# Retention and a mixture of experts: blocks of 768 slots with products of branched width, in place of blocks of 256

## The chip, the cores and the metric

The kernel runs on one core of a Trainium2 chip, in float32. The metric is the device time of one execution in microseconds (us). Each kernel ran in turn with the kernel before on the same chip. The experiments were made in three rounds, on chip 2, chip 3 and chip 2 again; across rounds, ratios and the block stages of the profiles compare better than times. A core's engines are named as in the profile: PE is the matrix engine (PEld its weight loads), DVE, ACT and POOL the vector, scalar and general engines, SP the engine that issues most transfers. PEq and the like are the profile's names for their sequencers.

## The reference

Retention over 8 sequences of 576 tokens (8 heads of 64) gives x with 512 features for each of 4608 tokens. A gate then picks one of 8 experts for each token, and the token goes through that expert's two matrices:

```python
for s in range(S):
    fresh_e = int(np.argmax(logits[b, s]))
    if s == 0 or local_gate[b, s] < 0.5:
        e = fresh_e
    else:
        e = prev_e if prev_e >= 0 else fresh_e
    prev_e = e
    ...                                        # p: softmax of the logits
    h = np.maximum(x[b, s] @ w1[e], 0.0)       # w1[e]: 512 x 1024
    out[b, s] = p[e] * (h @ w2[e])             # w2[e]: 1024 x 512
```

How many tokens an expert gets is known only when the kernel runs. With these inputs it is 652, 576, 581, 554, 591, 517, 606 and 531.

## The kernel before

Three stages follow each other: retention, which writes x to DRAM; routing, which gives each token a slot in a list that is sorted by expert; and the blocks, in which slots are gathered, go through their expert, and are scattered to their rows of the output. Each expert's tokens are padded to whole blocks of T = 256 slots. There are always as many blocks as any choice of experts can need, and nothing branches:

```python
T = 256
SUB = T // P                       # P = 128
NBLK = (NTOK - E) // T + E         # 25

for j in range(NBLK):
    e = nc.values_load(eid[0:1, j:j + 1], engines=[ET.SP], ...)
    w1s = weights.tile(...); w2s = weights.tile(...)      # two buffers each
    # cut: eight transfers of 512 KB, that expert's w1 and w2
    for u in range(SUB):
        # cut: gather 128 rows of x, transpose them on PE into PSUM (xgps)
        nc.vector.tensor_copy(xT[:, :, u * P:(u + 1) * P], xps)
    hT = mid.tile([P, FK, T], F32, name="hT")
    for m in range(0, FK, 2):                             # FK = 8
        hps = ps_h.tile([P, 2, T], F32, name="hps")
        for v in range(2):
            for c in range(DK):                           # DK = 4
                nc.tensor.matmul(hps[:, v, :], lhsT=w1s[:, m + v, c, :], rhs=xT[:, c, :], ...)
        nc.scalar.activation(hT[:, m:m + 2, :], hps, Act.Relu)
    for u in range(SUB):
        yps = ps_y.tile([P, D], F32, name="yps")
        for m in range(FK):
            nc.tensor.matmul(yps, lhsT=hT[:, m, u * P:(u + 1) * P], rhs=w2s[:, m, :], ...)
        nc.vector.tensor_scalar(y, yps, pslot[:, s:s + 1], None, Alu.mult)
        # cut: scatter y to its rows of out
```

Below, a "hidden product" is one into hps, an "output group" is the work on 128 slots into one yps tile, and a "seam" is the way from one block into the next.

Of the kernel before, what the change touches and what calls it, by code (L numbers as in the profile page):

```python
# [9 lines left out]
F32 = mybir.dt.float32  # L10
BF16 = mybir.dt.bfloat16
I32 = mybir.dt.int32
# [13 lines left out]
NTOK = B * S  # L26
NCH = NTOK // P  # chunks of 128 tokens
PER = 2 * S // P  # chunks in a pair of sequences
MID = PER // 2  # the chunk that ends one sequence and begins the next
HALF = S - P * MID  # L30
assert HALF == P // 2 and NTOK % (2 * S) == 0

T = 256  # tokens of one expert that go through its weights together
SUB = T // P
# Each expert's tokens are padded to whole blocks: what any choice of experts can need.
NBLK = (NTOK - E) // T + E
NSUB = NBLK * SUB
NOWHERE = 2 * NTOK  # the row of a slot without a token


@with_exitstack
def kernel(
# [23 lines left out]
    pslot = keep.tile([P, NSUB], F32, name="pslot")  # L66
    eid = keep.tile([1, NBLK], I32, name="eid")
    lt = keep.tile([P, NCH, E + 1], F32, name="lt")
    make_identity(nc, ident)

# [1 line left out]
    with ExitStack() as part:  # L72
# [12 lines left out]
        nc.scalar.dma_start(out=wg.rearrange("p k e -> p (k e)"), in_=wgl)  # L85
        # A key at partition p is seen from the queries at p and after.
        mask = once.tile([P, P], F32, name="mask")
# [44 lines left out]
        def outputs(i):  # L132
# [9 lines left out]
            if m > 0:  # L142
                # In the chunk of two sequences, only the first one's queries see what was before.
                n = HALF if m == MID else P
                for c in range(HP):
                    nc.tensor.matmul(  # L146
                        ops[0:n, 2 * c:2 * c + 2, :].rearrange("p h d -> p (h d)"),
                        lhsT=qT[:, c, 0:n], rhs=states[(i + 1) % 2][:, c, :],
                        start=False, stop=True, skip_group_check=True)
# [38 lines left out]

# [1 line left out]
    with ExitStack() as part:  # L190
# [12 lines left out]
        def for_all(t, n):  # L203
# [5 lines left out]
        one_of_sub = number("one_of_sub", [P, NSUB], [[1, NSUB]])  # L209
        one_of_blk = number("one_of_blk", [1, NBLK], [[1, NBLK]])  # L210
        token1 = number("token1", [P, NCH], [[P, NCH]], base=1, channel=1)
        place = number("place", [P, NCH], [[E * P, NCH]], base=1, channel=E)
# [10 lines left out]

        # The first of the greatest logits, and where the local gate asks for it.
        lg = lt[:, :, :E]
# [13 lines left out]
        nc.vector.memset(fr[HALF:HALF + 1, MID:NCH:PER], 1.0)  # L239
        # 8 * token + expert where it is asked for, -1 elsewhere: the last one that was is the  # L240
        # greatest until then.
        nc.vector.tensor_scalar(a, a, -1.0, float(E), Alu.mult, Alu.add)
# [29 lines left out]

        # Its share of the softmax.
        one = rt.tile([P, NCH, E], F32, name="one")
# [11 lines left out]

        # Tokens of each expert before each token: in its chunk, in the chunks before, and the
        # slots of the experts before.
        inside = ps_r.tile([P, NCH, E], F32, name="inside")
# [9 lines left out]
            cum.rearrange("p e c -> p (e c)"), going.rearrange("p e c -> p (e c)"),  # L299
            tot.rearrange("p e c -> p (e c)"), 0.0, Alu.mult, Alu.add)  # L300
        nb = rt.tile([P, E], F32, name="nb")
        nbi = rt.tile([P, E], I32, name="nbi")
        nc.vector.tensor_scalar(nb, cum[:, :, NCH - 1], float(T - 1), None, Alu.add)
        nc.vector.tensor_copy(nbi, nb)
        nc.vector.tensor_scalar(nbi, nbi, T.bit_length() - 1, None, Alu.arith_shift_right)
        nc.vector.tensor_copy(nb, nbi)
        last = rt.tile([P, E], F32, name="last")
        nc.vector.tensor_tensor_scan(last, nb, nb, 0.0, Alu.add, Alu.max)
        first = rt.tile([P, E], F32, name="first")
        nc.vector.tensor_tensor(first, last, nb, op=Alu.subtract)  # L310
        nc.vector.tensor_scalar(first, first, float(T), None, Alu.mult)
        nc.vector.tensor_tensor(cum, cum, tot, op=Alu.subtract)
        nc.vector.tensor_tensor(cum, cum, first.unsqueeze(2).to_broadcast([P, E, NCH]), op=Alu.add)
# [10 lines left out]

        # The expert of each block.
        past = rt.tile([1, NBLK, E], F32, name="past")
# [4 lines left out]
        nc.vector.tensor_scalar(eb, eb, float(E - 1), None, Alu.min)  # L331
        nc.vector.tensor_copy(eid, eb)

        # The token and the share of each slot: one product of the tokens' rows and columns.
        col = rt.tile([P, NCH, 2, NSUB], F32, name="col")
# [24 lines left out]

# [1 line left out]
    io = pool(ctx, "io", 4)  # L362
    mid = pool(ctx, "mid", 2)
    ps_x = pool(ctx, "ps_x", 2, PSUM)
    ps_h = pool(ctx, "ps_h", 3, PSUM)
    ps_y = pool(ctx, "ps_y", 3, PSUM)
    CUT = 4
    for j in range(NBLK):
        e = nc.values_load(eid[0:1, j:j + 1], engines=[ET.SP], min_val=0, max_val=E - 1,
                           skip_runtime_bounds_check_because="it is cut off there")  # L370
        w1s = weights.tile([P, FK, DK, P], F32, name="w1s")
        w2s = weights.tile([P, FK, D], F32, name="w2s")
        f = FK // CUT
        for t, src in ((w1s.rearrange("p m k f -> p (m k f)"), w1), (w2s.rearrange("p m d -> p (m d)"), w2)):
            for i in range(CUT):
                cols = slice(i * f * D, (i + 1) * f * D)
                nc.sync.dma_start(out=t[:, cols],
                                  in_=src[bass.ds(e, 1)].rearrange("o p x -> (o p) x")[:, cols])
        xT = mid.tile([P, DK, T], F32, name="xTs")
        for u in range(SUB):  # L380
            s = j * SUB + u
            xg = io.tile([P, D], F32, name="xg")
            nc.gpsimd.indirect_dma_start(  # L383
                out=xg, out_offset=None, in_=xd,
                in_offset=bass.IndirectOffsetOnAxis(ap=gidx[:, s:s + 1], axis=0))
            xps = ps_x.tile([P, DK, P], F32, name="xgps")
            for c in range(DK):
                nc.tensor.transpose(xps[:, c, :], xg[:, c * P:(c + 1) * P], ident)  # L388
            nc.vector.tensor_copy(xT[:, :, u * P:(u + 1) * P], xps)  # L389
        hT = mid.tile([P, FK, T], F32, name="hT")  # L390
        for m in range(0, FK, 2):
            hps = ps_h.tile([P, 2, T], F32, name="hps")
            for v in range(2):
                for c in range(DK):
                    nc.tensor.matmul(hps[:, v, :], lhsT=w1s[:, m + v, c, :], rhs=xT[:, c, :],  # L395
                                     start=(c == 0), stop=(c == DK - 1), skip_group_check=True)
            nc.scalar.activation(hT[:, m:m + 2, :], hps, Act.Relu)  # L397
        for u in range(SUB):
            s = j * SUB + u
            yps = ps_y.tile([P, D], F32, name="yps")  # L400
            for m in range(FK):
                nc.tensor.matmul(yps, lhsT=hT[:, m, u * P:(u + 1) * P], rhs=w2s[:, m, :],  # L402
                                 start=(m == 0), stop=(m == FK - 1))
            y = io.tile([P, D], F32, name="y")
            nc.vector.tensor_scalar(y, yps, pslot[:, s:s + 1], None, Alu.mult)  # L405
            nc.gpsimd.indirect_dma_start(  # L406
                out=out, out_offset=bass.IndirectOffsetOnAxis(ap=sidx[:, s:s + 1], axis=0),
                in_=y, in_offset=None, bounds_check=NTOK - 1, oob_is_err=False)


def _by_token(a, np):
    # (B, H, S, DH) -> (chunk, token, h d)
    return a.transpose(0, 2, 1, 3).reshape(NCH, P, D)


def _by_feature(a, np):
    # (B, H, S, DH) -> (chunk, d of two heads, pair token)
    x = a.transpose(0, 2, 1, 3).reshape(NCH, P, HP, P)
    return x.transpose(0, 3, 2, 1).reshape(NCH, P, D)


def _decay(np):
    """By each place in a pair of sequences and each head: what scales a query, and a key."""
    at = (np.arange(PER)[None, :] * P + np.arange(P)[:, None]) % S
    gamma = 1.0 - 2.0 ** (-5.0 - np.arange(H))
    power = gamma[None, None, :] ** at[:, :, None].astype(np.float64)
    both = np.stack([power / math.sqrt(DH), 1.0 / power], 1)
    return both.reshape(P, 2 * PER * H).astype(np.float32)
# [28 lines left out]
```

## Time and profile before

| | before |
|---|---|
| time, median of 3 runs | 1039.18 us (1037.77 to 1045.94) |
| PE busy, of a span of 1037.5 us | 974.9 us, 94% |
| first hidden product starts | 295.17 us |
| last output product ends | 1026.3 us |
| data moved | 166.03 MB |

The third and fourth rows frame the block stage: 731 us, which is 25 blocks of 29.25. Read the span first, then which engine is busy in each stretch. Here that is PE throughout the block stage, so a change there is worth the PE time it saves, less the PE idle time that it makes. The lines that carry this stand in the prediction.

### The profile page before, as it was taken

The page shows a single profiled execution, that of the slowest core. Times are in us where ns is not written, and L with a number is a line of the kernel's source. Part 1 is how long each engine was busy: PE and PEld are TensorE (multiplying, and loading weights), DVE is VectorE, ACT ScalarE, POOL GpSimd, SP SyncE. Part 2 cuts the span into 40 slices and gives each one's busy share as a digit, 9 for nine tenths or more (in the row PEclk, how much of TensorE's full clock was granted, in tenths as well). Part 3 has the DMA queues.
Part 4 walks back from the last instruction along what each step waited for, and adds up shares of the span by engine and source line. Part 5 has one row for each costly group of instructions (what it writes and reads, how often), then busy time and mean ns, then how long its engine had stood idle before and what let it go on. Part 6 is the DMA issues. An engine that isn't in the chain of part 4 may idle for free. (4 is left out here: it accounts for less than half of the span.)

```text
span 1037.5 us, 12062 instructions
## 1 busy us (share of the span) xinstructions
PE 974.9 (94%) x4918; PEld 719.0 (69%) x4918; DVE 166.8 (16%) x282; ACT 123.8 (12%) x238; POOL 140.7 (14%) x158
## 2 busy tenths in 40 slices
PE   7999999996479999999999999999999999999995
PEld 6999999995466666666666666666666666666662
DVE  2333332324711111010111111010111110010100
ACT  2222222221000000000000000000000000000000
POOL 2111111110021111011111110011111110110000
PEclk9999999998589999999999999999999999999998
DMA  5444444430735544555455544555455544555300
GB/s 201 154 158 157 151 163 162 163 133 32 273 122 203 201 156 148 185 197 177 153 179 187 193 156 153 181 193 188 138 187 203 164 158 160 195 183 167 127 2 0
DMA packets 47509, 166.03 MB, mean 160 GB/s; under 512 B 7006, under 2 KB 7134, under 8 KB 47456
## 3 DMA queue, kind: packets, MB, share of 16 engines
q1 hardware_dynamic: 39168, 142.62, 40.5%
q0 software_dynamic: 8000, 22.56, 6.3%
q8 instruction: 39, 0.64, 0.2%
q14 instruction: 14, 0.11, 0.0%
q10 hardware_dynamic: 288, 0.09, 0.0%
HBM read 146.37 MB, written 22.54 MB: 163 GB/s over the span
## 5 line engine op out<-in xcount | busy, mean ns | idle before, releaser
L395 PE MATMUL hps<-xTs,w1s 128*128 128x256 f32 x1600 | 353.2, 382 | 14.1 <-DVE xTs L389 14.1
L402 PE MATMUL yps<-w2s,hT 128*128 128x512 f32 x800 | 347.4, 592 | 0.0
L395 PEld LDWEIGHTS hps<-xTs,w1s 128*128 128x128 f32 x1600 | 303.0, 191 | 60.2 <-DVE xTs L389 19.8
L402 PEld LDWEIGHTS yps<-w2s,hT 128*128 128x128 f32 x800 | 152.0, 190 | 180.7 <-issue 179.4
L405 DVE TENSOR_SCALAR y<-yps,pslot 128x512 f32<-128x512 f32 x50 | 37.5, 751 | 665.4 <-PE yps L402 665.4
L397 ACT ACTIVATE hT<-hps 128x512 f32<-128x512 f32 x100 | 59.7, 597 | 700.2 <-PE hps L395 700.2
L406 POOL DMA_INDIRECT out_dram<-y,sidx x50 | 50.7, 1014 | 512.0 <-DVE y L405 505.3
L139 PE MATMUL ops<-vs,sT 128*128 128x64 f32 x576 | 82.3, 277 | 0.0
L139 PEld LDWEIGHTS ops<-vs,sT 128*128 128x128 f32 x576 | 72.4, 191 | 4.9 <-issue 0.6
L127 DVE TENSOR_TENSOR sT<-sps,mask 128x512 f32<-128x512 f32 x72 | 46.4, 686 | 159.9 <-PE sps L123 159.9
L383 POOL DMA_INDIRECT xg<-xd,gidx x50 | 48.7, 975 | 164.0 <-PE xgps L388 121.2
L116 POOL TENSOR_TENSOR vs<-ld,dec 128x512 f32<-128x512 f32 x36 | 37.5, 1042 | 190.0 <-PE kv L155 173.2
L123 PE MATMUL sps<-ld,kT 64*128 64x128 f32 x576 | 43.2, 288 | 0.2 <-DVE sT L127 0.2
L161 ACT COPY state<-kv 64x256 f32<-64x256 f32 x64 | 23.4, 366 | 160.2 <-PE kv L155 159.4
L176 PE MATMUL lps<-wg,xT 128*128 128x9 f32 x288 | 38.0, 259 | 1.5 <-ACT xT L174 1.1
L176 PEld LDWEIGHTS lps<-wg,xT 128*128 128x128 f32 x288 | 34.9, 191 | 5.2 <-ACT xT L174 4.7
L123 PEld LDWEIGHTS sps<-ld,kT 64*128 64x128 f32 x576 | 36.3, 190 | 2.9 <-DVE sT L127 0.4
L388 PEld LDWEIGHTS xgps<-ident,xg 128*128 128x128 f32 x200 | 24.2, 146 | 20.1 <-issue 19.5
L155 PE MATMUL kv<-vs,ld 128*128 128x128 f32 (+1 forms) x256 | 35.5, 281 | 0.5 <-ACT state L161 0.5
L146 PE MATMUL ops<-state,ld 128*128 128x128 f32 (+1 forms) x256 | 35.4, 281 | 0.0
L388 PE MATMUL xgps<-ident,xg 128*128 128x128 f32 x200 | 27.7, 282 | 6.6 <-DMA xg<-xd,gidx 6.6
L389 DVE COPY xTs<-xgps 128x512 f32<-128x512 f32 x50 | 32.2, 682 | 7.1 <-PE xgps L388 7.1
(112 smaller groups left out, 271.2 us busy)
## 6 DMA issues: line engine op xcount, KB each, us to landing
w1s<-in_w_dram SPq DMA_DIRECT2D x100, 512.0 KB, 5.5
w2s<-in_w_dram SPq DMA_DIRECT2D x100, 512.0 KB, 8.1
ld<-in_qkv_dram SPq DMA_DIRECT2D x36, 768.0 KB, 4.5
xd<-x SPq DMA_DIRECT2D x36, 256.0 KB, 2.2
xg<-xd,gidx POOLq DMA_INDIRECT x50, 7.3
out_dram<-y,sidx POOLq DMA_INDIRECT x50, 7.5
dec<-in_decay_dram ACTq DMA_DIRECT2D x1, 72.0 KB, 4.6
wg<-in_wgl_dram ACTq DMA_DIRECT2D x1, 18.0 KB, 6.2
```

The lines of the kernel that those rows point to most:

```text
L116: nc.gpsimd.tensor_tensor(vs.rearrange("p (h d) -> p h d", h=H), vn.rearrange("p (h d) -> p h d", h=H), dec[:, 1, m, :].unsqueeze(2).to_br ...
L123: nc.tensor.matmul(sps[u][:, c, :], lhsT=kT[r, c, :], rhs=qT[r, c, :], start=True, stop=True, skip_group_check=True)
L127: nc.vector.tensor_tensor(sT[:, u], sps[u], (mask2 if m == MID else mask).unsqueeze(1).to_broadcast([P, HP, P]), op=Alu.mult)
L139: nc.tensor.matmul(ops[:, h, :], lhsT=sT[:, h % 2, h // 2, :], rhs=vs[:, h * DH:(h + 1) * DH], start=(h == 0), stop=(m == 0), skip_group_c ...
L176: nc.tensor.matmul(lps[:, i, :], lhsT=xT[:, c, :], rhs=wg[:, c, :], start=(c == 0), stop=(c == DK - 1), skip_group_check=True)
L383: nc.gpsimd.indirect_dma_start(out=xg, out_offset=None, in_=xd, in_offset=bass.IndirectOffsetOnAxis(ap=gidx[:, s:s + 1], axis=0))
L388: nc.tensor.transpose(xps[:, c, :], xg[:, c * P:(c + 1) * P], ident)
L395: nc.tensor.matmul(hps[:, v, :], lhsT=w1s[:, m + v, c, :], rhs=xT[:, c, :], start=(c == 0), stop=(c == DK - 1), skip_group_check=True)
L397: nc.scalar.activation(hT[:, m:m + 2, :], hps, Act.Relu)
L402: nc.tensor.matmul(yps, lhsT=hT[:, m, u * P:(u + 1) * P], rhs=w2s[:, m, :], start=(m == 0), stop=(m == FK - 1))
L405: nc.vector.tensor_scalar(y, yps, pslot[:, s:s + 1], None, Alu.mult)
L406: nc.gpsimd.indirect_dma_start(out=out, out_offset=bass.IndirectOffsetOnAxis(ap=sidx[:, s:s + 1], axis=0), in_=y, in_offset=None, bounds_c ...
```

## The change

Padding 4608 tokens to blocks of 256 costs 25 x 256 = 6400 slots. The change uses one block of up to 768 slots for each expert and lets PE jump to products of about the width that the expert needs, so each expert's weights are also loaded once. A block's hidden products come in two passes of at most 384 columns. Each pass is written out in eight widths under a tree of branches. Output groups after the first stand under a branch of their own. Six blocks always run, and seven more are nested under branches on the number of blocks needed. The core of the diff:

```diff
-T = 256
+T = 768
 SUB = T // P
+PASS = T // 2
 NBLK = (NTOK - E) // T + E
+ALWAYS = -(-NTOK // T)                      # 6
+WIDTHS = (128, 192, 224, 256, 288, 320, 352, PASS)
 ...                                         # cut: routing also gives each block's token count
-    io = pool(ctx, "io", 4)
+    io = pool(ctx, "io", 2 * SUB)
+    hTs = [keep.tile([P, FK, T], F32, name=f"hT{i}") for i in range(2)]   # zeroed by POOL
+    def hidden(w1s, xT, hT, base, n):
+        for m in range(FK):
+            hps = ps_h.tile([P, PASS], F32, name="hps")
+            for c in range(DK):
+                nc.tensor.matmul(hps[:, 0:n], lhsT=w1s[:, m, c, :], rhs=xT[:, c, base:base + n], ...)
+            nc.scalar.activation(hT[:, m, base:base + n], hps[:, 0:n], Act.Relu)
+    def by_width(held, base, widths, body):
+        if len(widths) == 1:
+            body(widths[0])
+            return
+        h = len(widths) // 2
+        with tc.If(held > base + widths[h - 1]) as wider:
+            by_width(held, base, widths[h:], body)
+        with wider.Else():
+            by_width(held, base, widths[:h], body)
 ...
-        # the hidden products, 256 wide
+        by_width(held, 0, WIDTHS, lambda n: hidden(w1s, xT, hT, 0, n))
+        with tc.If(held > PASS):
+            by_width(held, PASS, WIDTHS, lambda n: hidden(w1s, xT, hT, PASS, n))
 ...
+            if u == 0:
+                product()
+            else:
+                with tc.If(held > u * P):
+                    product()
+    for j in range(ALWAYS):
+        block(j)
+    total = nc.values_load(plan[0:1, 2 * NBLK:], ...)
+    with ExitStack() as rest:
+        for j in range(ALWAYS, NBLK):
+            rest.enter_context(tc.If(total > j))
+            block(j)
```

In `by_width` the wide half of the tree stands first in the program. A pass of 192 or 224 columns therefore jumps over the wide half, and then over part of the narrow one.

More of the change, by code (lines that the diff above doesn't have):

```diff
@@ L66 @@
     pslot = keep.tile([P, NSUB], F32, name="pslot")
-    eid = keep.tile([1, NBLK], I32, name="eid")
+    plan = keep.tile([1, 2 * NBLK + 1], I32, name="plan")
     lt = keep.tile([P, NCH, E + 1], F32, name="lt")
@@ L210 @@
         one_of_blk = number("one_of_blk", [1, NBLK], [[1, NBLK]])
+        start_of_blk = number("start_of_blk", [1, NBLK], [[T, NBLK]])
+        full = number("full", [P, ALWAYS], [[T, ALWAYS]])
         token1 = number("token1", [P, NCH], [[P, NCH]], base=1, channel=1)
@@ L300 @@
             tot.rearrange("p e c -> p (e c)"), 0.0, Alu.mult, Alu.add)
+        count = cum[:, :, NCH - 1]
+        over = rt.tile([P, E, ALWAYS], F32, name="over")
+        nc.vector.tensor_tensor(over, count.unsqueeze(2).to_broadcast([P, E, ALWAYS]),
+                                full.unsqueeze(1).to_broadcast([P, E, ALWAYS]), op=Alu.is_gt)
         nb = rt.tile([P, E], F32, name="nb")
-        nbi = rt.tile([P, E], I32, name="nbi")
-        nc.vector.tensor_scalar(nb, cum[:, :, NCH - 1], float(T - 1), None, Alu.add)
-        nc.vector.tensor_copy(nbi, nb)
-        nc.vector.tensor_scalar(nbi, nbi, T.bit_length() - 1, None, Alu.arith_shift_right)
-        nc.vector.tensor_copy(nb, nbi)
+        nc.vector.tensor_reduce(nb, over, axis=AX.X, op=Alu.add)
         last = rt.tile([P, E], F32, name="last")
@@ L311 @@
         nc.vector.tensor_scalar(first, first, float(T), None, Alu.mult)
+        until = rt.tile([1, E], F32, name="until")
+        nc.vector.tensor_tensor(until, count[0:1], first[0:1], op=Alu.add)
         nc.vector.tensor_tensor(cum, cum, tot, op=Alu.subtract)
@@ L331 @@
         nc.vector.tensor_scalar(eb, eb, float(E - 1), None, Alu.min)
-        nc.vector.tensor_copy(eid, eb)
+        planf = rt.tile([1, 2 * NBLK + 1], F32, name="planf")
+        nc.vector.tensor_copy(planf[:, 0:NBLK], eb)
+        nc.vector.tensor_tensor(past, one_of_e[0:1].unsqueeze(1).to_broadcast([1, NBLK, E]),
+                                eb.unsqueeze(2).to_broadcast([1, NBLK, E]), op=Alu.is_equal)
+        nc.vector.tensor_tensor(past, past, until.unsqueeze(1).to_broadcast([1, NBLK, E]), op=Alu.mult)
+        held = planf[:, NBLK:2 * NBLK]
+        nc.vector.tensor_reduce(held, past, axis=AX.X, op=Alu.add)
+        nc.vector.tensor_tensor(held, held, start_of_blk, op=Alu.subtract)
+        nc.vector.tensor_scalar(held, held, 0.0, float(T), Alu.max, Alu.min)
+        nc.vector.tensor_copy(planf[:, 2 * NBLK:], last[0:1, E - 1:E])
+        nc.vector.tensor_copy(plan, planf)
         col = rt.tile([P, NCH, 2, NSUB], F32, name="col")
@@ L366, with block @@
     ps_y = pool(ctx, "ps_y", 3, PSUM)
+    hTs = [keep.tile([P, FK, T], F32, name=f"hT{i}") for i in range(2)]
+    for t in hTs:
+        nc.gpsimd.memset(t, 0.0)
     CUT = 4
-    for j in range(NBLK):
-        e = nc.values_load(eid[0:1, j:j + 1], engines=[ET.SP], min_val=0, max_val=E - 1,
+    def hidden(w1s, xT, hT, base, n):
+        for m in range(FK):
+            hps = ps_h.tile([P, PASS], F32, name="hps")
+            for c in range(DK):
+                nc.tensor.matmul(hps[:, 0:n], lhsT=w1s[:, m, c, :], rhs=xT[:, c, base:base + n],
+                                 start=(c == 0), stop=(c == DK - 1))
+            nc.scalar.activation(hT[:, m, base:base + n], hps[:, 0:n], Act.Relu)
[8 more added lines that the diff above has]
+            by_width(held, base, widths[:h], body)
+    def block(j):
+        e = nc.values_load(plan[0:1, j:j + 1], engines=[ET.SP], min_val=0, max_val=E - 1,
                            skip_runtime_bounds_check_because="it is cut off there")
+        held = nc.values_load(plan[0:1, NBLK + j:NBLK + j + 1], engines=[ET.PE, ET.Activation, ET.DVE, ET.Pool],
+                              min_val=0, max_val=T,
+                              skip_runtime_bounds_check_because="it is cut off there")
         w1s = weights.tile([P, FK, DK, P], F32, name="w1s")
@@ L389 @@
             nc.vector.tensor_copy(xT[:, :, u * P:(u + 1) * P], xps)
-        hT = mid.tile([P, FK, T], F32, name="hT")
-        for m in range(0, FK, 2):
-            hps = ps_h.tile([P, 2, T], F32, name="hps")
-            for v in range(2):
-                for c in range(DK):
-                    nc.tensor.matmul(hps[:, v, :], lhsT=w1s[:, m + v, c, :], rhs=xT[:, c, :],
-                                     start=(c == 0), stop=(c == DK - 1), skip_group_check=True)
-            nc.scalar.activation(hT[:, m:m + 2, :], hps, Act.Relu)
+        hT = hTs[j % 2]
@@ L398 @@
+        by_width(held, 0, WIDTHS, lambda n: hidden(w1s, xT, hT, 0, n))
+        with tc.If(held > PASS):
+            by_width(held, PASS, WIDTHS, lambda n: hidden(w1s, xT, hT, PASS, n))
         for u in range(SUB):
             s = j * SUB + u
-            yps = ps_y.tile([P, D], F32, name="yps")
-            for m in range(FK):
-                nc.tensor.matmul(yps, lhsT=hT[:, m, u * P:(u + 1) * P], rhs=w2s[:, m, :],
-                                 start=(m == 0), stop=(m == FK - 1))
-            y = io.tile([P, D], F32, name="y")
@@ L405, with product @@
-            nc.vector.tensor_scalar(y, yps, pslot[:, s:s + 1], None, Alu.mult)
-            nc.gpsimd.indirect_dma_start(
-                out=out, out_offset=bass.IndirectOffsetOnAxis(ap=sidx[:, s:s + 1], axis=0),
-                in_=y, in_offset=None, bounds_check=NTOK - 1, oob_is_err=False)
+            def product(u=u, s=s):
+                yps = ps_y.tile([P, D], F32, name="yps")
+                for m in range(FK):
+                    nc.tensor.matmul(yps, lhsT=hT[:, m, u * P:(u + 1) * P], rhs=w2s[:, m, :],
+                                     start=(m == 0), stop=(m == FK - 1))
+                y = io.tile([P, D], F32, name="y")
+                nc.vector.tensor_scalar(y, yps, pslot[:, s:s + 1], None, Alu.mult)
+                nc.gpsimd.indirect_dma_start(
+                    out=out, out_offset=bass.IndirectOffsetOnAxis(ap=sidx[:, s:s + 1], axis=0),
+                    in_=y, in_offset=None, bounds_check=NTOK - 1, oob_is_err=False)
@@ L411, in _by_token @@
+            if u == 0:
[5 more added lines that the diff above has]
+        block(j)
+    total = nc.values_load(plan[0:1, 2 * NBLK:], min_val=0, max_val=NBLK,
+                           skip_runtime_bounds_check_because="it is their sum")
+    with ExitStack() as rest:
+        for j in range(ALWAYS, NBLK):
+            rest.enter_context(tc.If(total > j))
+            block(j)
 def _by_token(a, np):
```

## The prediction

> **What bounds the kernel now.** I read the page's busy shares and slices first, then the costliest groups, the stretches by stage, the waits of TensorE (PE), and the timeline of one block.
>
> The shares and the clock:
>
> ```profile
> PE 974.9 (94%) x4918; PEld 719.0 (69%) x4918; DVE 166.8 (16%) x282; ACT 123.8 (12%) x238; POOL 140.7 (14%) x158
> ...
> PE   7999999996479999999999999999999999999995
> ...
> PEclk9999999998589999999999999999999999999998
> ```
>
> PE is busy from end to end except in slices 10 and 11. Three stages follow from the line numbers: retention to 250 us, the choice of experts (routing) to 294, the blocks of slots to 1028, then an end:
>
> ```profile
> 0.00:250.00 250.00, 241.28 (x2240) 227.72 (x2240) 71.98 (x110) 63.67 (x137) 38.91 (x46) 1.00 0.46 153
> 250.00:294.00 44.00, 15.66 (x89) 13.57 (x88) 27.91 (x74) 0.44 (x1) 7.37 (x17) 0.58 0.57 211
> 294.00:1028.00 734.00, 717.95 (x2592) 477.70 (x2592) 66.92 (x99) 59.70 (x100) 94.08 (x95) 1.00 0.48 162
> 1028.00:1037.50 9.50, 0.00 (x0) 0.00 (x0) 0.00 (x0) 0.00 (x0) 0.39 (x1) 0.69 0.00 0
> ```
>
> Columns: stretch, its length, busy us of PE, PEld, DVE, ACT, POOL, then granted clock, DMA share, GB/s. In the third row PE works 718 of 734 us; no other engine exceeds 94 apart from the overlapped weight load, and the DMA is half used. So the block stage costs what its PE work costs. Its two groups:
>
> ```profile
> L395 PE MATMUL hps<-xTs,w1s 128*128 128x256 f32 x1600 | 353.2, 382 | 14.1 <-DVE xTs L389 14.1
> L402 PE MATMUL yps<-w2s,hT 128*128 128x512 f32 x800 | 347.4, 592 | 0.0
> ```
>
> Each product of the program gives two MATMUL records here (25 blocks x 32 x 2 = 1600). The mean of 382 ns is a latency, not a price: starts are what counts. One block in order of time:
>
> ```profile
> 324.02 1.04 PE L388 MATMUL xgps<-ident,xg 128*128 128x128 f32 x8
> 324.21 1.93 SPq L377 DMA_DIRECT2D w2s<-in_w_dram  x4
> 324.22 0.75 DVE L405 TENSOR_SCALAR y<-yps,pslot 128x512 f32<-128x512 f32 x1 [6.12 <-PE yps L402]
> 324.89 1.28 DVE L389 COPY xTs<-xgps 128x512 f32<-128x512 f32 x2
> ...
> 325.62 14.08 PE L395 MATMUL hps<-xTs,w1s 128*128 128x256 f32 x64 [0.57 <-DVE xTs L389]
> ...
> 339.54 13.90 PE L402 MATMUL yps<-w2s,hT 128*128 128x512 f32 x32
> ...
> 353.27 1.04 PE L388 MATMUL xgps<-ident,xg 128*128 128x128 f32 x8
> ```
>
> From starts: transposes 1.60 (with 0.57 of waiting for the DVE copy), hidden products 13.92, output products 13.73; together 29.25 us a block, and 25 blocks are 731. A hidden MATMUL is 13.92/64 = 217.5 ns at 256 columns, an output MATMUL 13.73/32 = 429 ns at 512. The line through both is 6 ns + 0.826 ns per column. Pairs of 128 columns with a fresh weight load start about 111 ns apart in retention (eight kv records from 227.37 to 228.26 us), so down to some 128 columns streaming, not the load, sets the price.
>
> [...] The kernel before takes no such jumps; its page shows only that q8 fetched 39 packets with 0.64 MB, which is 16 KB each and fits PE's roughly 9,836 instructions. It does not show a stall's length. [...]clock 0.58 in routing, and the first hidden group after it took 15.28 us against 14.08.
>
> **The change, part by part.** I worked the tokens per expert out of the inputs: 652, 576, 581, 554, 591, 517, 606, 531 (4608). At T = 256 these need 25 blocks. At T = 768 there are 8 blocks, each a pass of 384 and a second of 288 (once), 224 (three) or 192 (four); 128-token output groups are 6 once and 5 seven times, 41. The other five of 13 blocks are skipped.
>
> - Hidden products: 64 MATMULs a pass. 384: 323 ns, 20.7 us, eight times 165. 288: 244 ns, 15.6. 224: 191 ns, 12.2, three times 37. 192: 165 ns, 10.5, four times 42. Sum 260, against 25 x 13.92 = 348: -88.
> - Output products: 41 against 50 groups of 6.87 us: 281 against 343: -62.
> - Transposes: 48 groups against 50, now in clusters of up to six on two PSUM buffers, so at the copies' pace (1.28/2 = 0.64 us): 31 against 25 x 1.60 = 40: -9. Their wait for DVE before each hidden pass goes, since in the scheduled order the next block's transposes mostly stand a pass ahead.
> - Weights: 8 x 4 MiB instead of 25. The DMA was not the bound: 0, but no rival either.
> - Routing: slots grow from 50 to 78 groups. The three DVE operations on col took 2.03 us for 1800 elements; at 2808 some 3.2, +3.4 on the path before the first slot product. The 72 slot MATMULs widen from 100 to 156 columns: +2.5. About ten more small DVE operations for the plan at 0.2 us, partly replacing four old ones: +1. Sum +7.
> - First block: its order has four gathers and transposes before the hidden pass instead of two, gathers 1.25 us apart: +2.5[...].
> - Blocks 6 and 7 stand under branches, and eight are needed. Nothing of them is ordered before the branch, on any engine: gathers follow the last output of the block before, and all six transposes precede its hidden pass. From PE's last product: DVE 0.2 + 0.75, scatter issue 0.28 + 0.98, [...]gather to transpose 3.6 (287.82 to 291.43 in routing), five more gathers at 1.25, transpose, copy and wait 1.4: near 15 us of which 4 are counted as transposes above. Add 2 for the cold clock[...]: +13, twice: +26.
> - Jumps of PE: a variant is 32 products x 4 records = 128 instructions, 8 KiB[...], so the trees hold eight variants, 64 KiB each. A block leaves the first tree over 56 KiB, enters the second over 32 and again over 8 or 16, and leaves over 8 or 16: up to four missed pages. An estimate of one miss, from the 2.2 us to landing of the xd issue and some 0.85 us for 16 KB in q8 (0.2% of 16 engines' span over 39): 3 us. [...]The two into the second tree follow a short queue (output products of 4 to 6 us), the last a queue of 165 ns pairs. I take 3 us shown per block: +24.
> - The sixth output group is untaken in seven blocks, and the untaken arm waits for PE's own last product: 0.5 each: +4.
> - Leaving the nested branches, at the end: +4.
>
> Sum: 1039 - 88 - 62 - 9 + 7 + 4 + 26 + 24 + 4 + 4 = 949; I say 952, since jumps are likelier to be dearer than cheaper.
>
> **The rivals.** A: fetch stalls are the new bound. If no miss is hidden, 32 x 3 = 96 us instead of 24: 1021, about nothing gained. For it: drained queues after the untaken arm[...]. [...]B: POOL becomes the bound: under branches scatters wait for all earlier scatters, and gathers stand behind them in one order. A scatter took 2.1 us of DMA after 1 us of issue in the tail of the chain, against 6.9 us per output group; I expect nothing, but if gathers came late each block would add 5: 990. C: all control flow hides, and the two joins cost only the gathers: 920. D: the padding saved is as computed but narrow MATMULs are bound by weight loads: PEld shows 191 ns each, although loads start closer than that. If 165 became 191 in the four narrow passes, +7.
>
> **Range and chances.** PE work falls by 159 us, which is 15%, on an engine 98% busy in that stage; this is nearly certain. Overheads of 30 (C) to 130 (A with B in part) leave 910 to 1010; eight in ten lie in 920 to 1000. Faster by 2% means under 1018: 0.92. Within: 0.06. Slower needs 180 us of overhead: 0.02.
>
> **What would show it.** Right: hps records 1024 with busy near 260 us in the forms 384, 288, 224 and 192; yps 656 with about 285; two PE idle stretches of 12 to 16 us ended by gathers, none at the first five seams; idle of PE just ahead of the second pass and behind it put down to "issue", 2 to 4 us a block; more q8 packets than 39 per executed instruction. Wrong: idle inside a pass, waiting for ACT; gathers as releaser at every seam; half clock in many slices; or a wait of PE on DVE before each output group.

Its sum came to 949 and was said as 952, and 4.5 us of it belong to estimates: 1.5 for a register load in the first block (its +4 is 2.5 and 1.5), and 1.5 for branches and a register load at each of the two joins (part of the near 15). At the first join the changed kernel's trace has 2.13 us between the end of the scatter's issue and the first gather's, put down to "issue". The other terms can be set against traces. By "such jumps" taken branches of PE are meant. A variant's 8 KiB follows from the packets of queue q8: 0.64 MB for 9,836 instructions is 65 bytes each. The 2 us for a cold clock are an estimate beside the 1.2 between 15.28 and 14.08 us. That 3 us would show per block was the author's estimate too, taken at the price of one miss; what was held against rival A, that queued products hide stalls, no trace showed then.

## The result

The changed kernel took 952.54 us in the median of 4 runs (951.05 to 953.35); the kernel before took 1039.33 beside it. The ratio is 0.916, with a 95% interval of 0.913 to 0.919. Ratios here are the mean time of one kernel's runs over that of the other's runs of the same rounds, so they are not quite the ratio of the medians quoted.

The page of the changed kernel: shares, slices, one DMA queue, and the two groups of products (busy us, mean ns of one, then the idle time just ahead of them with what ended it).

```profile
PE 845.8 (89%) x4190; PEld 586.6 (62%) x4190; DVE 164.6 (17%) x277; ACT 118.1 (12%) x266; POOL 138.2 (15%) x151
...
PE   7999999999627999999989979999998959969892
...
PEclk9999999999857999999999989999998979988996
...
q8 instruction: 82, 1.34, 0.6%
...
L396 PE MATMUL hps<-xTs,w1s 128*128 128x384 f32 (+3 forms) x1024 | 272.2, 429 | 21.7 <-issue 21.7
L446 PE MATMUL yps<-w2s,hT 128*128 128x512 f32 x656 | 285.1, 593 | 0.6 <-PEq L457 0.6
```

The products are 1024 and 656 records, as counted beforehand. PE is still the busiest engine by far, but now has gaps. Those ahead of hidden products are not waits for data: "issue" means that PE waited for nothing the profile shows. The q8 packets, 16 KB of instructions each, went from 39 to 82. (The recorded texts call such a packet a page.)

The block stage and a little of the end, from the stretches by stage (length, busy us of PE, PEld, DVE, ACT and POOL, granted clock, DMA share, GB/s):

```profile
302.00:943.00 641.00, 584.66 (x1859) 341.56 (x1857) 60.22 (x86) 53.90 (x128) 80.28 (x83) 0.96 0.22 74
```

The first hidden product starts at 302.47 and the last output product ends at 933.8. So routing and the first gathers became 7.3 us longer, the block stage 99.8 shorter (731.1 to 631.3), and the end 5.8 longer (11.2 to 17.0). The sum is -86.7, the difference of the two spans. Within the block stage PE's busy time fell by 133 us (718.0 to 584.7). Its idle time rose from 14.1 to 47.1, once the edges of the windows are taken off.

What the 47.1 are can be read off PE's timeline (start, length, group, and in brackets the idle time ahead of it). Four stretches of it:

```profile
374.92 38.83 PE L446 MATMUL yps<-w2s,hT 128*128 128x512 f32 x90
413.59 10.56 PE L396 MATMUL hps<-xTs,w1s 128*128 128x192 f32 x64
...
481.00 6.17 PE L446 MATMUL yps<-w2s,hT 128*128 128x512 f32 x14
490.80 33.01 PE L396 MATMUL hps<-xTs,w1s 128*128 128x224 f32 x128 [3.62 <-issue]
...
637.77 6.17 PE L446 MATMUL yps<-w2s,hT 128*128 128x512 f32 x14
644.77 33.01 PE L396 MATMUL hps<-xTs,w1s 128*128 128x224 f32 x128 [0.82 <-issue]
...
708.51 5.39 PE L446 MATMUL yps<-w2s,hT 128*128 128x512 f32 x12 [0.30 <-PEq L457]
718.36 13.60 PE L396 MATMUL hps<-xTs,w1s 128*128 128x192 f32 x64 [4.46 <-issue]
731.80 29.35 PE L446 MATMUL yps<-w2s,hT 128*128 128x512 f32 x68
770.25 3.84 PE L434 MATMUL xgps<-ident,xg 128*128 128x128 f32 x16 [9.11 <-DMA xg<-xd,gidx]
...
777.09 20.88 PE L396 MATMUL hps<-xTs,w1s 128*128 128x384 f32 x64 [0.27 <-issue]
```

The last three lines are the way into block 6, the first one under a branch on the number of blocks. PE idles until gathers land: 15.9 us from the last product to the first hidden one, of which about 10 are idle. Block 7 repeats it with 15.3 and 9. These two seams are called the joins below. The other lines show the entry to a second pass. In block 1, behind 38.8 us of queued output products, it costs nothing. In blocks 2 to 5, behind 4.5 to 6.2 us of them, it costs from 0.82 to 4.85. (Each "x128" is a second pass and the next block's first.) With 1.7 ahead of first passes, all such gaps come to the 21.7 of the page. With 19 at the two joins, 5.5 of waits for DVE's copies ahead of transposes and 0.6 after untaken branches, 46.8 of the 47.1 are found.

The granted clock during a narrow pass (same columns as above; clock third from the end):

```profile
413.59:424.15 10.56, 10.56 (x66) 10.56 (x65) 0.00 (x0) 2.32 (x7) 0.00 (x0) 1.00 0.39 139
490.80:503.00 12.20, 12.20 (x64) 12.20 (x65) 0.00 (x0) 2.50 (x7) 0.00 (x0) 1.00 0.01 3
718.36:731.90 13.54, 13.54 (x65) 13.54 (x66) 0.00 (x0) 2.32 (x7) 0.00 (x0) 0.78 0.01 2
```

The first and third are passes of the same 192 columns. The third followed 4.46 us of idle time, ran at a mean clock of 0.78 and took 3 us longer. The second followed 3.62 us of idle time and kept its clock. The length of the gap alone does not tell: in block 7 half clock for 3.41 us, from 891.6 on, followed a gap of 2.69 and one of 0.31 came within it. So a gap can cost twice: once as idle time, and once in the products behind it.

### The profile page after: what moved, and what is told of

It reads as the page before. It is cut to its first block, busy times and chain, and to the rows that moved or that the text cites. A ratio compares the mean times of both kernels' runs of the same rounds, so it can differ in the third digit from the quotient of the medians.

```text
span 950.8 us, 10793 instructions
## 1 busy us (share of the span) xinstructions
PE 845.8 (89%) x4190; PEld 586.6 (62%) x4190; DVE 164.6 (17%) x277; ACT 118.1 (12%) x266; POOL 138.2 (15%) x151
## 5 line engine op out<-in xcount | busy, mean ns | idle before, releaser
L396 PE MATMUL hps<-xTs,w1s 128*128 128x384 f32 (+3 forms) x1024 | 272.2, 429 | 21.7 <-issue 21.7
L446 PE MATMUL yps<-w2s,hT 128*128 128x512 f32 x656 | 285.1, 593 | 0.6 <-PEq L457 0.6
L396 PEld LDWEIGHTS hps<-xTs,w1s 128*128 128x128 f32 x1024 | 195.4, 198 | 99.7 <-issue 31.5
L446 PEld LDWEIGHTS yps<-w2s,hT 128*128 128x128 f32 x656 | 123.7, 190 | 150.8 <-issue 149.5
L398 ACT ACTIVATE hT<-hps 128x384 f32<-128x384 f32 (+3 forms) x128 | 53.9, 421 | 594.8 <-PE hps L396 594.8
L449 DVE TENSOR_SCALAR y<-yps,pslot 128x512 f32<-128x512 f32 x41 | 30.8, 751 | 484.1 <-PE yps L446 484.1
L450 POOL DMA_INDIRECT out_dram<-y,sidx x41 | 40.8, 994 | 413.5 <-DVE y L449 364.5
L429 POOL DMA_INDIRECT xg<-xd,gidx x48 | 46.2, 962 | 181.2 <-PE xgps L434 127.0
L434 PE MATMUL xgps<-ident,xg 128*128 128x128 f32 x192 | 36.0, 327 | 31.8 <-DMA xg<-xd,gidx 26.0
```

Of the source, the lines that this page charges most:

```text
L396: nc.tensor.matmul(hps[:, 0:n], lhsT=w1s[:, m, c, :], rhs=xT[:, c, base:base + n], start=(c == 0), stop=(c == DK - 1))
L398: nc.scalar.activation(hT[:, m, base:base + n], hps[:, 0:n], Act.Relu)
L429: nc.gpsimd.indirect_dma_start(out=xg, out_offset=None, in_=xd, in_offset=bass.IndirectOffsetOnAxis(ap=gidx[:, s:s + 1], axis=0))
L434: nc.tensor.transpose(xps[:, c, :], xg[:, c * P:(c + 1) * P], ident)
L450: nc.gpsimd.indirect_dma_start(out=out, out_offset=bass.IndirectOffsetOnAxis(ap=sidx[:, s:s + 1], axis=0), in_=y, in_offset=None, bounds_c ...
```

## The experiments

Theory 1 is the prediction's: jumps into the trees need instruction packets that have yet to be fetched (a miss), and a miss shows where few products are queued. I took this to be so because an untaken output group, whose arm waits for PE's own last product, has just drained PE; the prediction itself had only a queue of 4 to 6 us, and named the drain under its rival A. Theory 2 is its rival: the gaps at second passes have another cause, such as waits at the branches themselves or a wait for w1, and the number of jumps doesn't matter. Each edit is made to the changed kernel. Where no other run is named, times are compared with its 952.5. The kernel before took 1039.4, 1042.8 and 1039.2 us in the three rounds of experiments.

### The sixth output group second

Only one expert has more than 640 tokens, so group 5 is skipped seven times, as the last one before the next block. Moving it forward puts products between the drain and the next jump.

```diff
-        for u in range(SUB):
+        for u in (0, SUB - 1, *range(1, SUB - 1)):
```

> Only the order of the output groups of a block changes: 0, 5, 1, 2, 3, 4 instead of 0 to 5, so that the untaken arm of the sixth group, which waits for TensorE's own last product, has four groups (27 us of queued products) after it. Theory (drained queue): the page jumps into the second tree are exposed because that wait empties the queue just before them. Then idle ahead of hidden products falls from 21.7 us to 5 to 8 (blocks 6 and 7, whose queue is short for another reason, keep 2 to 3 each), the narrow passes lose their half-clock start, and the time falls from 952 to 925 to 935. Rival (each jump stalls TensorE whatever is queued): idle stays near 21 us and the time within 5 us of 952.

Measured: 945.58 us (940.19 to 950.71), ratio 0.910. Idle ahead of hidden products fell only from 21.7 to 18.2. One of the gaps that stayed:

```profile
532.32 32.02 PE L446 MATMUL yps<-w2s,hT 128*128 128x512 f32 x74 [0.35 <-PEq L457]
564.17 1.14 PE L396 MATMUL hps<-xTs,w1s 128*128 128x192 f32 x6
569.05 12.40 PE L396 MATMUL hps<-xTs,w1s 128*128 128x192 f32 x58 [3.74 <-issue]
```

PE had 32 us of products since the drain and still stood for 3.74 us, six records into the pass. In the packets of the trace, instructions came at 557.6, 560.7 and 566.7: the first two while products were left, the third too late. (In the changed kernel 0.98 us show at the same place, behind a packet at 566.2.) At the entry that had cost 3.62 us, the drain lay 36 us back and the gap was 4.01. So the drain is not what makes these gaps. This part of Theory 1 fell. Nor does a long queue hide every chain of fetches: behind 32 us and more of products (here, in block 5 of this run, and in block 1 of the changed kernel) the chain's first fetch, after 18 us and more without one, came only 6.7 to 6.8 us before they ended.

### Eight blocks always

```diff
-ALWAYS = -(-NTOK // T)
+ALWAYS = 8
```

> Eight blocks instead of six stand ahead of the nested branches; these inputs need eight, so the executed work is the same, and only the two seams in front of blocks 6 and 7 become like the first five. Theory: each of those seams costs TensorE 15 to 16 us, of which 4 are transposes that stay; the new seams get the fetch stalls of the others (up to 5 us against 2.5 now). 952 becomes 928 to 936. Rival (the seam's wait is for weights or something else that returns): at most 8 us gained, 944 or more, and a new releaser at the seams.

Measured: 933.51 us (932.28 to 935.44), ratio 0.899. The two joins cost 19.0 us net. The gaps at second passes are a matter of their own, as they stayed: 24.4 us of idle time ahead of hidden products, all of it "issue".

### One width alone

Every pass is 384 wide. The trees are gone; the branches on the second pass, on output groups and on blocks stay.

```diff
-WIDTHS = (128, 192, 224, 256, 288, 320, 352, PASS)
+WIDTHS = (PASS,)
```

> No width trees: both passes are always 384 columns wide, the second under one branch. What the choice of width is worth: eight second passes of 20.7 us (165) against the 103.7 us of busy time that they have now, +62; the fetch stalls ahead of hidden products (21.7 us) mostly go, -18; half-clock starts are in the 103.7 already. 952 becomes 985 to 1003. Rival (jumps and trees cost about what the narrower passes save): 945 to 965.

Measured: 991.91 us (989.78 to 995.71), ratio 0.955. Page lines of this run:

```profile
q8 instruction: 37, 0.61, 0.2%
...
L396 PE MATMUL hps<-xTs,w1s 128*128 128x384 f32 x1024 | 336.7, 489 | 3.4 <-issue 3.4
```

With the trees went all the gaps at second passes (the 3.4 lie in block 0, of which more below), while branches and drains were still there. Against the changed kernel, choosing the width saves 336.7 - 272.2 = 64.5 us of products. It gives back 18.3 as added idle time ahead of them, and 39.4 are left in the medians. By the block stages the sum closes: without the choice PE's busy time there is 59.0 longer (records of neighbouring groups overlap, so this is less than 64.5), its idle time 20.8 shorter, and the stage 38.2 longer.

### The narrow arms first in the second tree

The arms are the same and the number of branches taken differs little, but passes of 192 and 224 columns no longer jump over the wide half.

```diff
+    def by_width_up(held, base, widths, body):
+        ...
+        with tc.If(held <= base + widths[h - 1]) as narrower:
+            by_width_up(held, base, widths[:h], body)
+        with narrower.Else():
+            by_width_up(held, base, widths[h:], body)
-            by_width(held, PASS, WIDTHS, lambda n: hidden(w1s, xT, hT, PASS, n))
+            by_width_up(held, PASS, WIDTHS, lambda n: hidden(w1s, xT, hT, PASS, n))
```

> The second tree tests from the narrow end, so that the taken variants are reached over one skip of 8 KiB (192) or 16 KiB (224) instead of two skips of 32 and 8 or 16 KiB; the same products, branches and waits. Theory (missed instruction pages at some 3.3 us each, as the fetches of queue q8 at 484.7, 488.4 and 491.9 us suggest): one miss fewer per block, idle ahead of hidden products falls from 21.7 to 4 to 9 us, time 930 to 940. Rival (the stall is the wait of the drained engine and the branches themselves, not pages): idle stays near 20 us, time 948 to 955.

Measured: 932.16 us (930.27 to 936.02), ratio 0.897. Its two groups on the page:

```profile
L456 PE MATMUL yps<-w2s,hT 128*128 128x512 f32 x656 | 285.7, 593 | 5.6 <-issue 3.5
L396 PE MATMUL hps<-xTs,w1s 128*128 128x384 f32 (+3 forms) x1024 | 267.3, 423 | 3.0 <-ACT hT L398 1.9
```

And the entry to the 224 pass that had waited 3.62 us, on PE's timeline:

```profile
481.61 6.17 PE L456 MATMUL yps<-w2s,hT 128*128 128x512 f32 x14
487.62 12.27 PE L396 MATMUL hps<-xTs,w1s 128*128 128x224 f32 x64
```

Both kernels have 6.17 us of output products ahead of this pass; with the short jump nothing shows. The instruction packets show why: between the start of these output products and the first hidden one, the changed kernel fetched 2, 2, 1 and 2 of them in blocks 2 to 5, this one 1, 1, 1 and 0. (The one with a single fetch in the changed kernel is block 4, whose gap was 0.82 us behind the same 6.17.) Idle time fell by 18.7 ahead of hidden products and rose by 5.0 ahead of output products. A narrow arm that stands first has a longer way out of the tree; that this is the cause was not tested. The hidden products became 4.9 us shorter: the 192 passes that had stood behind gaps, at 0.72 to 0.86 of the clock, all take 10.56 us now. Theory 2 fell: the gaps go with the instruction packets fetched at jumps.

### All output groups always

This takes away the branches on output groups, and with them their drains, at the price of seven more groups (7 x 6.87 = 48 us).

```diff
-            if u == 0:
+            if u >= 0:
```

> All six output groups of a block without a branch: 48 instead of 41 groups, seven more of 6.87 us (+48); the branches and the waits of the untaken arms go (0.3 us each). If output groups cost PE time alone, 952 becomes 993 to 1001. Rival (the branches of the output groups cost much, and keep the engine from running ahead, so most of what they save they give back): under 980.

Measured: 998.16 us (993.92 to 1001.57), ratio 0.955: 45.6 slower, about the price of the groups. But idle time ahead of hidden products rose to 29.7, in fewer places. Two of them on PE's timeline:

```profile
410.99 0.60 PE L434 MATMUL xgps<-ident,xg 128*128 128x128 f32 x4
411.42 1.02 PE L446 MATMUL yps<-w2s,hT 128*128 128x512 f32 x2
421.14 13.43 PE L396 MATMUL hps<-xTs,w1s 128*128 128x192 f32 x64 [8.69 <-issue]
...
500.66 6.17 PE L446 MATMUL yps<-w2s,hT 128*128 128x512 f32 x14
508.48 33.01 PE L396 MATMUL hps<-xTs,w1s 128*128 128x224 f32 x128 [1.65 <-issue]
```

This gives the size of the thing. Instruction packets came at 415.1, 418.2 and 421.6 around the first gap, and the pass began between the second and the third. Entering the second tree is a chain of such fetches, 3.1 to 3.9 us apart ahead of the gaps that I looked at (5.9 twice in the sixth-group run). What shows is the chain less the products queued by then: behind 1.6 us of products 8.69 show, behind 6.17 only 1.65. Queued products and gap together make 7 to 10.5 us where a gap shows, here and in blocks 2 to 5 of the changed kernel. At the first gap transposes stand just ahead of the jump, with 1.6 us of products behind the last of them (410.99); whether they hold the fetches back was not shown. So what counts is not a drain, but how many packets the jump needs and how much work is queued at it.

### A third buffer for w2

By the trace, SP starts the next expert's w2 load when the last output group has freed its buffer, 5 to 9 us ahead of the second tree. In the changed kernel's timeline of SP:

```profile
479.05 1.91 SPq L423 DMA_DIRECT2D w2s<-in_w_dram  x4
...
708.33 1.90 SPq L423 DMA_DIRECT2D w2s<-in_w_dram  x4
```

About 1.3 us later the DMA engines are busy almost without a break (96% from 480.3 to 488.4, 98% from 709.8 to 715.0), and instruction fetches fall among that (at 484.7 and 488.4, and at 711.9). A third buffer moves that load away, to where w1's is.

```diff
+    weights2 = pool(ctx, "weights2", 3)
-        w2s = weights.tile([P, FK, D], F32, name="w2s")
+        w2s = weights2.tile([P, FK, D], F32, name="w2s")
```

> Three buffers instead of two for the second weights, so their load no longer starts when the last output group of the block before ends, 5 to 9 us ahead of the second tree, but with the first weights after the second pass. Products, branches and pages stay. Theory (contention: the page fetches of TensorE stand behind 2 MB of weights on the same DMA engines): idle ahead of hidden products falls from 21.7 to 8 to 16 us, time 938 to 948. Rival (a page takes its 3.3 us whatever else moves): idle 19 to 24, time 949 to 956.

Measured: 942.25 us (938.61 to 950.95), ratio 0.904. One of its four runs is about as slow as the changed kernel, so the time alone is weak evidence. The page line is clearer:

```profile
L397 PE MATMUL hps<-xTs,w1s 128*128 128x384 f32 (+3 forms) x1024 | 272.0, 428 | 14.7 <-issue 14.7
```

With the same jumps, idle time fell from 21.7 to 14.7, and the longest gap from 4.85 to 2.9. The block stage became 7.0 us shorter (631.3 to 624.3), all of it idle time. About a third of the gaps (7.0 of 21.7 us) was contention with that load. What it delayed was the start of the chain: in blocks 2 to 5 the first packet came 3.4 to 4.2 us after the output products ahead of the pass had begun, and 0.9 to 1.2 us after without the load; the next packets followed no faster on the whole. The entry that had cost 3.62 us:

```profile
481.01 6.17 PE L447 MATMUL yps<-w2s,hT 128*128 128x512 f32 x14
488.76 33.02 PE L397 MATMUL hps<-xTs,w1s 128*128 128x224 f32 x128 [1.57 <-issue]
```

### The two remedies together

Narrow arms first, and eight blocks always.

> The narrow-first second tree and the eight unconditional blocks together. If pages and seams are separate costs, the savings of 20 and 19 us add: 910 to 917. Rival (they share the stalls of the last two blocks, or the new seams expose new pages): 920 to 930.

Measured: 912.23 us (907.14 to 912.95), ratio 0.873. In time the two gains seem to add up (20.4 and 19.0 of 952.5 would give 913.1), but that is partly luck: this trace is one of the two in which full clock came late. The block stage became 45.7 us shorter (631.3 to 585.6), where the remedies alone took off 17.9 and 19.8. With eight blocks in a row there are two more seams whose gaps the narrow arms remove: against eight blocks always, idle time ahead of hidden products fell from 24.4 to 4.0, and the products themselves from 271.3 to 262.5.

### And the first pass without a tree

Every expert has over 384 tokens here, so the first tree always took its widest arm.

```diff
-        by_width(held, 0, WIDTHS, lambda n: hidden(w1s, xT, hT, 0, n))
+        hidden(w1s, xT, hT, 0, PASS)
```

> As before, and the first pass always 384 wide without a tree, which these inputs take anyway: eight exits over 56 KiB less and the first pass free for the scheduler. In the trace the exits were hidden behind the 384 pass, with 0.7 us shown now and then, so 0 to 5 us are gained: 907 to 916. Rival (its exits and register load cost more than the trace shows): under 904.

Measured: 900.40 us (898.95 to 906.92), ratio 0.863, and right for any inputs, though an expert with few tokens would compute unneeded columns. Its page:

```profile
q8 instruction: 60, 0.98, 0.4%
...
L456 PE MATMUL yps<-w2s,hT 128*128 128x512 f32 x656 | 286.2, 593 | 4.3 <-issue 4.3
L396 PE MATMUL hps<-xTs,w1s 128*128 128x384 f32 (+3 forms) x1024 | 262.8, 416 | 0.0
```

It gained 11.8 in the medians; my theory's range ended at 907, and the median lies under the rival's 904. But the runs of this round seem to be of two kinds, with the late full clock and without, and the medians mix them: the two profiled runs, which both have it, took 912.95 and 906.92, 6.0 apart. Their block stages differ by 7.6 (585.6 to 578.0). Of that, 4.7 are idle time, 4.0 of it the last ahead of hidden products; the rest I did not trace. So the gain is 6 to 8 us, a little above my range of 0 to 5, and the rival is not shown. This is the best of the versions run.

### All of it with the third buffer

> Narrow-first second tree, eight unconditional blocks, the first pass always whole, and three buffers for the second weights. With the first three nearly all stalls ahead of hidden products had gone (4.3 us of issue left, ahead of output products), so the third weight buffer has little left to save: 893 to 902. Rival (the weight load that starts at the end of the output groups still costs its 10 us): under 892.

Measured: 905.71 us (905.22 to 905.87), ratio 0.871. This missed its range from above, and is no gain on 900.40. The block stage is 5.4 us longer (583.4 against 578.0), 3.3 of it idle time and 2.1 busy time. Its one gap ahead of hidden products is in block 0, on the timelines of PE and ACT:

```profile
304.92 9.84 PE L397 MATMUL hps<-xTs,w1s 128*128 128x384 f32 x30
317.68 0.49 ACT L399 ACTIVATE hT<-hps 128x384 f32<-128x384 f32 x1 [10.13 <-remote]
318.22 12.25 PE L397 MATMUL hps<-xTs,w1s 128*128 128x384 f32 x32 [3.46 <-issue]
```

ACT does one activation at 307.06 and its next at 317.68, so the three hps buffers fill and PE stands; half clock for 3.41 us follows. That is about the whole difference, so with no gap left ahead of second passes the third buffer was worth nothing. The version with one width has such a gap there too (3.4 us), and so has the next run. What ACT waited for I could not tell.

### No blocks that are not needed

This kernel is right for these inputs only. It shows what the five skipped blocks cost in routing (48 instead of 78 slot columns) and at the end. It is compared with eight blocks always, at 933.5.

```diff
-NBLK = (NTOK - E) // T + E
-ALWAYS = -(-NTOK // T)
+NBLK = 8
+ALWAYS = 8
```

> Right for these inputs alone: eight unconditional blocks and no further ones, so no nested branches at the end and 48 slot groups instead of 78. Against the eight-block kernel's 933.5: the end after the last product shortens from 17 to some 11 us (-6), and the col operations and slot products in routing shrink (three operations of 1728 instead of 2808 elements, -3.7; narrower slot products, -1): 920 to 926. Rival (the end's length is the last scatter's landing and not the branches): 927 to 931.

Measured: 929.73 us (926.96 to 938.61), ratio 0.895. Both ends did what was expected: the first hidden product started 3.8 us earlier (297.5 against 301.3), and from the last product to the end it took 11.3 us instead of 17.7. But the block stage became 9.4 us longer in the profiled runs (611.5 to 620.9). Idle time ahead of hidden products is 28.4 us against 24.4, and the products themselves took 276.5 against 271.3. The longest gap is 6.3 us, and there is a wait for ACT of 3.1 in block 0. So the total lies in the rival's range for another reason than the rival's. Why the gaps changed was not shown.

## Why the prediction was right

The time, 952.5, is 0.5 us from the 952.0 predicted. Part of that is luck: terms of the sum erred in both directions. (One reading was wrong without harm: at 256 slots these counts need 24 blocks, not 25, but the kernel before runs 25 in any case.) In us:

| term | predicted | measured |
|---|---|---|
| hidden products | -88 | about -78 |
| output products | -62 | -62 |
| transposes, with waits for copies | -9 | about -1.5 |
| joins before blocks 6 and 7 | +26 | about +20 |
| gaps at jumps | +24 | +21.7 |
| untaken output groups | +4 | +0.6 |
| routing and first block | +11 | +7.3 |
| end | +4 | +5.8 |

The measured column sums to -86, against -90 predicted; the time of 952 had taken 3 us off that gain beforehand.

- **Hidden products.** The price per column held. From start to start an undisturbed record of 192 columns took 10.40/64 = 163 ns (165 predicted) and one of 384 took 20.71/64 = 324 (323). So the rival in which weight loads set the price fell. The term was too hopeful by some 10 us because it priced all passes at full clock. By form, three of the four were:

```profile
L396 PE MATMUL hps<-xTs,w1s 128*128 128x384 f32 x512 | 169.0, 491 | 1.7 <-issue 1.7
L396 PE MATMUL hps<-xTs,w1s 128*128 128x192 f32 x256 | 50.9, 367 | 13.3 <-issue 13.3
L396 PE MATMUL hps<-xTs,w1s 128*128 128x224 f32 x192 | 37.1, 354 | 6.7 <-issue 6.7
```

  The four 192 passes took 50.9 instead of 42; three of them stand behind gaps and started at a low clock, while the one without a gap took 10.56. The prediction counted the clock at the joins, but not behind its own 3 us gaps.

- **Output products** went as counted: 41 groups, 656 records.

- **Transposes** were taken at the pace of DVE's copies alone, 31 us. In the block stage they kept PE for some 33 us (what its busy time leaves beside the other two groups, counted from starts) and waited 5.5 more, 38.5 in all. At the joins a group took 1.09 us, not 0.64.

- **Joins.** The place, the releaser (gathers) and the length held: 15.9 and 15.3 us, predicted near 15, and none at the first five seams. More of that length was transposes than I had set aside, so idle time and cold clock come to about 20 instead of 26. The idle stretches of 12 to 16 us that were named as a sign came as 10.4 and 8.9, each in pieces. Taking the branches away from blocks 6 and 7 gave back 19.0.

- **Gaps at jumps.** The mechanism held, and so did the sum, 21.7 against 24; by block it was 0 to 5.8 us, where 3 had been set for each. A packet, estimated at 3 us, came every 3.1 to 3.9. The mechanism was shown by changing only the order of the arms (idle time from 21.7 to 3.0). The short queue that the prediction named, 4 to 6 us of output products, was there (4.5 to 6.2). The drain by the untaken group, which it named under rival A and I took up in the experiments, was not the reason: with it moved 32 us away a gap of 3.74 stayed, and with all drains removed the gaps grew. What shows is a chain of fetches less the products queued at the jump, and about a third of what shows (7.0 of 21.7 us) is contention with the w2 load. I had also spread the misses over all blocks and behind passes; in the changed kernel the large ones all lie at the entry to the second pass.

- **Untaken output groups** cost 0.30 us where they show at all, which is twice.

- **Routing.** The growth from 50 to 78 groups and the longer first block had been priced at 11, and 7.3 came. Of these, 3.8 were given back when five unneeded blocks were left out of the plan.

The rival in which all misses show (1021) fell because most are covered by queued products: 62 instruction packets came in the changed kernel's block stage, and 21.7 us of gaps show. The one in which control flow is free (920) fell by the two joins and the gaps. The one with late gathers fell because PE's gather waits stood at the two joins only.

## What to carry to other kernels

Price a branch on PE not by the branch but by what the jump reads: what showed here is a chain of instruction fetches, 3.1 to 3.9 us apart, less the work queued ahead (up to 7 us of it), so put the likely arm first, keep that much work queued ahead of the jump, start no large load just then (7.0 us here), and give up variants that the data don't need. A branch around a whole block costs what the scheduler may no longer move ahead of it; here two such joins cost 19 us, as much as the badly ordered tree. Compare the block stages of profiles too: here full clock came late in two runs, and their block stages began some 8 us later. And when a prediction meets its number, check its terms: here errors of 10 and 7 us were hidden by others of the opposite sign.
